# One fused attention-and-mixing kernel on one core: chunk states summed in PSUM, operations over two PSUM banks, and a new list scheduler

## The chip, the cores and the metric

The kernel runs on one core of one Trainium2 chip. The metric is the device time of one execution in microseconds (us), as a median of several runs. Engines are named as in the profile: PE is the matrix engine, PEld its weight loads, DVE the vector engine, ACT the scalar engine, POOL the GpSimd engine, SP the engine that issues most of the transfers. PE's results go to PSUM, a memory of eight banks here; the other tiles lie in SBUF, and an evacuation is a copy from PSUM to SBUF. "Clock" is the mean clock that the throttle granted PE, as a share of full speed; a run whose clock or time puts it in a slower state is labelled slow and is not compared.

## The reference

Two stages, one after the other. The first is a linear-attention recurrence with a decaying state per head, the second mixes tokens and channels.

```
# 4 batches, 8 heads, 768 tokens, head size 48
for t in range(S):
    cur     = outer(u * k[t], v[t])
    y[t]    = r[t] @ (state + cur)              # per head, 48 x 48 state
    state   = w * state + outer(k[t], v[t])
x = y with its heads side by side                # (4, 768, 384)

theta = x @ w_theta                              # 384 x 384
y2 = w_tok_r @ (x * cos(theta)) + w_tok_i @ (x * sin(theta))    # 768 x 768 over tokens
z  = x + y2
out = z + max(z @ w_ch, 0)
```

The recurrence is computed in six chunks of 128 tokens. With r multiplied by powers of w and k by inverse powers, a chunk is a masked product of transposed r and k ("scores", then `mAT`) plus a product with the state at the chunk's start (`Sb`).

## The kernel before

A Python planner (`Plan`) collects tasks with rough durations, orders them for each engine, and gives PSUM banks to them; the instructions are then emitted in that order. The framework adds the semaphore waits by what tiles each instruction touches. The parts that matter here:

```
P = Plan(8)
bank_t = [ps.tile([C, 512], F32, name=f"bank{i}") for i in range(8)]    # eight tiles of one bank

def flip6(dst, blocks, tok, prio, rd, wr):                # transposes on PE, one evacuation on ACT
    def go():
        for i, s in enumerate(blocks):
            nc.tensor.matmul(bank16(tok)[:, i * C:(i + 1) * C], s, ident, is_transpose=True, ...)
    P.add(PE, 55 * n, go, ...)
    P.add(ACT, act_ns(n * C), lambda: nc.scalar.activation(
        dst, bank16(tok)[:, :n * C].rearrange("p (a c) -> p a c", a=n), Act.Copy), ...)

# RT: transposed r of one batch and head pair. Partition p of r holds tokens 6p .. 6p+5,
# so block n of the transposes holds tokens n, n+6, n+12, ...
flip6(RT[:, hp].rearrange("q (p n) -> q n p", n=NCH), [Rw[:, n, 2 * hp:2 * hp + 2, :] for n in range(NCH)], ...)
```

Block n's 128 columns are written to `RT` at steps of six bf16 elements, 12 bytes. The reader of PSUM goes through consecutive elements, the writer of SBUF jumps.

```
# state of each chunk: kept in SBUF as fp32 (Y), updated on DVE, scaled to bf16 (Sb) on POOL
for hp in range(HP):
    nc.vector.scalar_tensor_tensor(Y[:, cc, hp, :], Y[:, cc - 1, hp, :], wC[:, hp:hp + 1],
                                   src[:, hp], op0=Alu.mult, op1=Alu.add)
P.add(POOL, ..., lambda: nc.gpsimd.tensor_mul(Sb[:, cc], Y[:, cc], wide(wC, D)), ...)

# theta, sin, cos, zr, channel product and fin: per chunk of 128 tokens, one bank each
# [... cut ...]

# startup: w broadcast to 128 partitions by a transfer; Ln of w, then Ln of the small wu tile,
# then the powers wpow (Exp), which wait for both
P.add(ACT, 150, lambda: nc.scalar.activation(lw_p, wup[:, :HP], Act.Ln), rd=["wup", "lw_f"], wr=["lw_p"], ...)
P.add(ACT, 500, lambda n=n: nc.scalar.activation(wpow[:, :, n, :], lw_f, Act.Exp, scale=tok_f[:, n:n + 1]),
      rd=["lw_f", "lw_p", "tok_f"], ...)
```

Of the kernel before, what the change touches and what calls it, by code (L numbers as in the profile page):

```python
# [15 lines left out]
F32 = mybir.dt.float32  # L16
# [4 lines left out]

def bc(ap, axis, n):
    new_ap = [list(x) for x in ap.ap]
    new_ap.insert(axis, [0, n])
    return dataclasses.replace(ap, ap=new_ap)


PE, DVE, ACT, POOL, SP = "PE", "DVE", "ACT", "POOL", "SP"


class Task:
    __slots__ = ("eng", "ns", "fn", "deps", "prio", "seq", "lat", "acq", "uses", "nwait",
                 "users", "ready", "end", "mode")


class Plan:



    def __init__(self, nbanks):  # L40
        self.tasks, self.writer, self.readers = [], {}, {}
        self.nbanks = nbanks
        self.bank_uses = {}
        self.bank_of = {}

    def add(self, eng, ns, fn, rd=(), wr=(), prio=0.0, lat=60.0, acq=(), use=(), mode=None):
        t = Task()
        t.eng, t.ns, t.fn, t.prio, t.lat, t.mode = eng, ns, fn, prio, lat, mode
        t.seq = len(self.tasks)
        t.acq, t.uses = list(acq), list(acq) + list(use)  # L50
        rd, wr = list(rd) + list(use), list(wr) + list(acq)
# [19 lines left out]

    def order(self):
# [5 lines left out]
        waiting = {e: [] for e in (PE, DVE, ACT, POOL, SP)}  # L78
        for t in self.tasks:
            if t.nwait == 0:  # L80
                waiting[t.eng].append(t)
        free_at = {e: 0.0 for e in waiting}
        last_mode = None
        banks = [(0.0, i) for i in range(self.nbanks)]
        left = dict(self.bank_uses)
        freed = {}
        out, now, n = [], 0.0, len(self.tasks)
        while len(out) < n:
            for e in waiting:
                while free_at[e] <= now:  # L90
                    nfree = sum(1 for b in banks if b[0] <= now)
                    best = None
                    for t in waiting[e]:
                        if t.ready <= now and len(t.acq) <= nfree:
                            if best is None or (t.prio, t.seq) < (best.prio, best.seq):
                                best = t
# [3 lines left out]
                    waiting[e].remove(t)  # L100
                    banks.sort()
                    for b in t.acq:
                        self.bank_of[b] = banks.pop(0)[1]
                    ns = t.ns
                    if e == PE:
                        if t.mode != last_mode:
                            ns += 100.0
                        last_mode = t.mode
                    free_at[e] = now + ns
                    t.end = now + ns + t.lat  # L110
                    out.append(t)
                    for b in t.uses:
                        left[b] -= 1
                        freed[b] = max(freed.get(b, 0.0), t.end)
                        if left[b] == 0:
                            banks.append((freed[b], self.bank_of[b]))
                    for x in t.users:
                        x.ready = max(x.ready, t.end)
                        x.nwait -= 1
                        if x.nwait == 0:  # L120
                            waiting[x.eng].append(x)
            nxt = [f for f in free_at.values() if f > now]
            nxt += [t.ready for e in waiting for t in waiting[e] if t.ready > now]
            nxt += [b[0] for b in banks if b[0] > now]
# [3 lines left out]
            now = min(nxt)  # L128
        return out


def rows_of(w, n):
    return dataclasses.replace(w, ap=[[0, n]] + [list(x) for x in w.ap])


def wide(ap, n):
    return dataclasses.replace(ap, ap=[list(x) for x in ap.ap] + [[0, n]])


@with_exitstack  # L140
def kernel(
# [13 lines left out]
    nc = tc.nc  # L155
    B, H, S, D = r.shape
# [7 lines left out]
    NS = NCH - 1  # L164
# [4 lines left out]
    bank_t = [ps.tile([C, 512], F32, name=f"bank{i}") for i in range(8)]  # L169

    def bank(tok):
        return bank_t[P.bank_of[tok]]

    def bank16(tok):
        return bank(tok).bitcast(BF16)
# [3 lines left out]


    ident_f = sb.tile([C, C], F32, name="ident_f")
    ident = sb.tile([C, C], BF16, name="ident")
    mask01 = sb.tile([C, C], BF16, name="mask01")
    pi2 = sb.tile([C, 1], F32, name="pi2")
    wu = sb.tile([2 * HP, 2, Dp], F32, name="wu")
    w_f = sb.tile([C, H, D], F32, name="w_f")
    lw_f = sb.tile([C, H, D], F32, name="lw_f")
    lw_p = sb.tile([C, HP], F32, name="lw_p")
    tok_i = sb.tile([C, NCH + 1], mybir.dt.int32, name="tok_i")
    tok_f = sb.tile([C, NCH + 1], F32, name="tok_f")  # L190
    wpow = sb.tile([C, H, NCH, D], F32, name="wpow")
    wpinv = sb.tile([C, H, D], F32, name="wpinv")
    wup = sb.tile([C, 2 * HP], F32, name="wup")
    wC = sb.tile([C, HP], F32, name="wC")
    uw = sb.tile([C, HP, 2], BF16, name="uw")

    NL = 8
    Ls = ring(NL, [C, 2 * HD], F32, "ld")
    r_fs = ring(2, [C, H, NCH * D], F32, "r_f")
    Rws = ring(1, [C, NCH, H, Dp], BF16, "Rw")  # L200
    Kws = ring(4, [C, 2, H, Dp], BF16, "Kw")
    vbs = ring(5, [C, 2, H, D], BF16, "vb")
# [3 lines left out]
    mATs = ring(6, [C, 2, HP, C], BF16, "mAT")  # L206
    Ys = ring(1, [C, NS, HP, D], F32, "Y")
    Sbs = ring(2, [C, NS, HP, D], BF16, "Sb")
    dgs = ring(3, [C, 2 * H], F32, "dg")
    yds = ring(3, [C, 2, H, D], BF16, "yd")  # L210
    xs = ring(3, [C, NCH, HD], BF16, "x")
# [3 lines left out]
    xTs = ring(2, [C, 2, ND, C], BF16, "xT")  # L215
    uns = ring(2, [C, 2, HD], BF16, "un")
    uTs = ring(2, [C, 2, ND, C], BF16, "uT")
# [6 lines left out]
    def act_ns(n, psum=True):  # L224
        return n / 1.2 + (60 if psum else 95)

    def dve_ns(n, rate=1.0):
        return n / (0.96 * rate) + 75

    def pool_ns(n):  # L230
        return 190 + 1.95 * n


    def setup():
        P.add(ACT, 100, lambda: nc.scalar.dma_start(out=w_f, in_=rows_of(w, C)),
              wr=["w_f"], prio=-100, lat=3000)

        def wu_fill():
            nc.vector.memset(wu, 0.5)
        P.add(DVE, 100, wu_fill, wr=["wu"], prio=-100)  # L240

        def wu_load():
            nc.scalar.dma_start(out=wu[:HP, :, :D], in_=w.rearrange("(a b) d -> a b d", b=2))
            nc.scalar.dma_start(out=wu[HP:, :, :D], in_=u.rearrange("(a b) d -> a b d", b=2))
        P.add(ACT, 200, wu_load, wr=["wu"], prio=-99, lat=3000)

        def tok():
            nc.gpsimd.iota(tok_i[:, :NCH], pattern=[[1, NCH]], base=0, channel_multiplier=NCH)
            nc.gpsimd.iota(tok_i[:, NCH:], pattern=[[0, 1]], base=0, channel_multiplier=1)
        P.add(POOL, 400, tok, wr=["tok_i"], prio=-100)  # L250

        def tok2():
            nc.vector.tensor_scalar(tok_i[:, :NCH], tok_i[:, :NCH], C - 1, None,
                                    op0=Alu.bitwise_and)
            nc.vector.tensor_copy(tok_f, tok_i)
            nc.vector.tensor_scalar(tok_f[:, NCH:], tok_f[:, NCH:], -1.0, -1.0,
                                    op0=Alu.mult, op1=Alu.add)
            nc.vector.memset(pi2, math.pi / 2.0)
            nc.vector.memset(uw, 0.0)
        P.add(DVE, 400, tok2, rd=["tok_i"], wr=["tok_f", "uw", "pi2"], prio=-99)  # L260

        def pads(ts):
            for t in ts:
                nc.gpsimd.memset(t[:, :, :, D:], 0.0)
        P.add(POOL, 900, lambda: make_identity(nc, ident_f), wr=["ident_f"], prio=-98)
        P.add(DVE, 200, lambda: nc.vector.tensor_copy(ident, ident_f), rd=["ident_f"],
              wr=["ident"], prio=-98)
        P.add(POOL, 600, lambda: pads(Rws), wr=[("Rw", hp) for hp in range(HP)], prio=-97)
        P.add(POOL, 800, lambda: pads(Kws), wr=[("Kw", i) for i in range(4)], prio=-96)

        def mask():
# [4 lines left out]
        P.add(POOL, 600, mask, wr=["mask"], prio=-95)  # L276

        P.add(ACT, 1800, lambda: nc.scalar.activation(lw_f, w_f, Act.Ln), rd=["w_f"],
              wr=["lw_f"], prio=-98)

        def wu_flip():
            nc.tensor.matmul(bank("wu")[:, :2 * HP], wu.rearrange("p a d -> p (a d)"),  # L282
                             ident_f[:2 * HP, :2 * HP], is_transpose=True,
                             start=True, stop=True)
        P.add(PE, 300, wu_flip, rd=["wu", "ident_f"], acq=["wu"], prio=-90)
        P.add(DVE, 100, lambda: nc.vector.tensor_copy(wup, bank("wu")[:, :2 * HP]),
              use=["wu"], wr=["wup"], prio=-90)
        P.add(ACT, 150, lambda: nc.scalar.activation(lw_p, wup[:, :HP], Act.Ln),
              rd=["wup", "lw_f"], wr=["lw_p"], prio=-97)

        def uw_fill():
# [3 lines left out]
        P.add(DVE, 200, uw_fill, rd=["wup"], wr=["uw"], prio=-90)  # L295
        for n in range(NCH):
            P.add(ACT, 500 + (1300 if n == 0 else 0), lambda n=n: nc.scalar.activation(  # L297
                wpow[:, :, n, :], lw_f, Act.Exp, scale=tok_f[:, n:n + 1]),
                rd=["lw_f", "lw_p", "tok_f"], wr=[("wpow", n)], prio=-96 + 0.1 * n)
        P.add(ACT, 500, lambda: nc.scalar.activation(  # L300
            wpinv, lw_f, Act.Exp, scale=tok_f[:, NCH:]),
            rd=["lw_f", "lw_p", "tok_f"], wr=["wpinv"], prio=-95)
        P.add(ACT, 150, lambda: nc.scalar.activation(wC, lw_p, Act.Exp, scale=float(C)),
              rd=["lw_p"], wr=["wC"], prio=-94)


    nload = [0]

    def slot():
        nload[0] += 1  # L310
# [349 lines left out]
```

## Time and profile before

| | before |
|---|---|
| time, median of 3 runs | 206.19 us (205.81 to 206.32) |
| span in the profile | 204.4 us |
| granted clock | 0.921 |
| PE busy | 145.3 us, 71% |
| DVE, ACT, POOL busy | 124.6, 123.3, 75.1 us |
| 16 RT evacuations | 46.0 us, 2874 ns each |
| first scores start | 26.98 us |

These are lines of the profile page of the kernel before: the busy time of each engine (share of the span, number of instructions), busy tenths in 40 equal slices for PE and ACT and the granted clock in tenths, the chain of waits that ended last (share of the span by engine, then by line), and groups of instructions (output, input, shapes, count, busy us, mean ns of one, idle time before them and its releaser).

```profile
span 204.4 us, 4137 instructions
...
PE 145.3 (71%) x1641; PEld 95.7 (47%) x1641; DVE 124.6 (61%) x260; ACT 123.3 (60%) x165; POOL 75.1 (37%) x73
...
PE   0008178896582897599933988999329989999971
...
ACT  2299987999599706409999433755992327511120
...
PEclk9999999999669589969995899999985999999998
...
PE 41%; ACT 21%; DVE 19%; issue 8%; DMA 8%; POOL 1%; ACTq 0%; POOLq 0%; DVEq 0%; SPq 0%
...
L382 ACT ACTIVATE xT_135<-bank_65 128x768 bf16<-128x768 bf16 x2 | 1.6, 810 | 11.0 <-PE bank_65 L379 11.0
...
L382 ACT ACTIVATE RT_104<-bank_63 128x768 bf16<-128x768 bf16 x2 | 5.9, 2946 | 0.0
```

Read the last two together: the same line of code, engine, operation, types and size, 810 against 2946 ns (all 12 `xT` evacuations take 827 ns on average, all 16 `RT` evacuations 2874). The input pattern is the same; only the output differs, consecutive for `xT` and in steps of 12 bytes for `RT`. The chain has no single owner: ACT has only 21% of it. But the slices show that ACT's 9s and PE's holes go together.

Windows of ten microseconds of the kernel before make that plain. The columns are the window, its length, busy us and number of instructions for PE, PEld, DVE, ACT and POOL, the granted clock, DMA share and GB/s.

```profile
core 0: us, PE busy (x) PEld busy (x) DVE busy (x) ACT busy (x) POOL busy (x), PEclk, DMA share, GB/s
...
20.00:30.00 10.00, 4.38 (x88) 3.59 (x84) 4.15 (x10) 9.77 (x9) 2.31 (x3) 1.00 0.20 74
...
60.00:70.00 10.00, 4.76 (x61) 2.88 (x61) 3.44 (x8) 10.00 (x8) 0.79 (x3) 0.81 1.22 241
...
100.00:110.00 10.00, 3.56 (x71) 2.88 (x68) 5.65 (x11) 10.00 (x5) 7.77 (x7) 0.86 0.76 138
...
140.00:150.00 10.00, 4.99 (x88) 3.99 (x85) 2.89 (x9) 9.58 (x5) 1.01 (x2) 1.00 0.19 72
```

Four times, once for each batch, ACT is full and PE is less than half busy. The first of them also ends the startup. This is the first score matmul in the timeline of the kernel before; the bracket says how long PE was idle and what released it:

```profile
26.98 0.28 PE L438 MATMUL bank_61<-RT_104,KT_106 64*128 64x128 bf16 x1 [5.62 <-ACT KT_106 L382]
```

The ACT queue had four RT evacuations of about 2.9 us in front of that `KT` evacuation.

### The profile page before, as it was taken

The page shows a single profiled execution, that of the slowest core. Times are in us where ns is not written, and L with a number is a line of the kernel's source. Part 1 is how long each engine was busy: PE and PEld are TensorE (multiplying, and loading weights), DVE is VectorE, ACT ScalarE, POOL GpSimd, SP SyncE. Part 2 cuts the span into 40 slices and gives each one's busy share as a digit, 9 for nine tenths or more (in the row PEclk, how much of TensorE's full clock was granted, in tenths as well). Part 3 has the DMA queues.
Part 4 walks back from the last instruction along what each step waited for, and adds up shares of the span by engine and source line. Part 5 has one row for each costly group of instructions (what it writes and reads, how often), then busy time and mean ns, then how long its engine had stood idle before and what let it go on. Part 6 is the DMA issues. An engine that isn't in the chain of part 4 may idle for free.

```text
span 204.4 us, 4137 instructions
## 1 busy us (share of the span) xinstructions
PE 145.3 (71%) x1641; PEld 95.7 (47%) x1641; DVE 124.6 (61%) x260; ACT 123.3 (60%) x165; POOL 75.1 (37%) x73
## 2 busy tenths in 40 slices
PE   0008178896582897599933988999329989999971
PEld 0016165774460555356621755657215655566630
DVE  2028279355740899978861999944419896544442
ACT  2299987999599706409999433755992327511120
POOL 6024121606960489523791083440104082400000
PEclk9999999999669589969995899999985999999998
DMA  4999209999899992829290510022020002022222
GB/s 119 236 230 227 112 6 275 333 332 321 170 198 292 189 167 50 263 69 203 81 195 0 129 29 3 0 82 77 0 77 3 0 3 77 3 77 77 79 80 77
DMA packets 60092, 25.25 MB, mean 124 GB/s; under 512 B 50472, under 2 KB 58536, under 8 KB 60072
## 3 DMA queue, kind: packets, MB, share of 16 engines
q1 hardware_dynamic: 59904, 24.78, 49.9%
q8 instruction: 13, 0.21, 0.5%
q10 hardware_dynamic: 168, 0.20, 0.5%
q14 instruction: 7, 0.06, 0.1%
HBM read 20.25 MB, written 4.72 MB: 122 GB/s over the span
## 4 chain that ended last, share of the span: by engine, by line
PE 41%; ACT 21%; DVE 19%; issue 8%; DMA 8%; POOL 1%; ACTq 0%; POOLq 0%; DVEq 0%; SPq 0%
ACT RT_104 L382 8%; ACT RT_105 L382 7%; DMA r_f_93<-in_r_dram 5%; PE bank_66 L586 5%; PE bank_64 L586 3%; DMA wu<-in_u_dram 3%; PE bank_68 L586 2%; PE bank_63 L586 2%; PE bank_65 L586 2%; DVE Y_116 L494 2%; DVE mAT_114 L443 2%; ACT wpow L297 2%; PE bank_67 L586 1%; PE bank_62 L586 1%; DVE Kw_96 L416 1%
## 5 line engine op out<-in xcount | busy, mean ns | idle before, releaser
L586 PEld LDWEIGHTS <-WrT 128*128 128x128 bf16 x144 | 14.5, 104 | 10.4 <-issue 3.1
L499 POOL TENSOR_TENSOR Sb_118<-Y_116,wC 128x192 bf16<-128x192 f32 x10 | 5.4, 544 | 34.0 <-DVE Y_116 L494 18.6
L586 PEld LDWEIGHTS <-WiT 128*128 128x128 bf16 x144 | 12.8, 98 | 6.8 <-issue 0.5
L397 POOL TENSOR_TENSOR Rw_94<-r_f_92,wpow 128x576 bf16<-128x576 f32 x6 | 10.1, 1713 | 10.1 <-ACT wpow L297 10.1
L397 POOL TENSOR_TENSOR Rw_94<-r_f_93,wpow 128x576 bf16<-128x576 f32 x8 | 12.6, 1600 | 0.4 <-DMA r_f_93<-in_r_dram 0.4
L499 POOL TENSOR_TENSOR Sb_117<-Y_116,wC 128x192 bf16<-128x192 f32 x10 | 6.1, 606 | 16.6 <-DVE Y_116 L494 13.5
L379 PEld LDWEIGHTS <-Rw_94 128*128 128x128 bf16 x96 | 8.0, 120 | 8.6 <-issue 6.2
L438 PEld LDWEIGHTS <-KT_107 64*128 64x128 bf16 x96 | 4.1, 116 | 12.4 <-issue 8.1
L449 DVE TENSOR_TENSOR PD_109<-RT_105,KT_107 128x1024 bf16<-128x1024 bf16 x4 | 3.3, 823 | 10.8 <-ACT RT_105 L382 6.6
L449 DVE TENSOR_TENSOR PD_108<-RT_104,KT_106 128x1024 bf16<-128x1024 bf16 x4 | 4.1, 1030 | 6.8 <-ACT KT_106 L382 6.8
L382 ACT ACTIVATE xT_135<-bank_65 128x768 bf16<-128x768 bf16 x2 | 1.6, 810 | 11.0 <-PE bank_65 L379 11.0
L438 PEld LDWEIGHTS <-KT_106 64*128 64x128 bf16 x96 | 3.8, 117 | 8.6 <-ACT KT_106 L382 5.9
L604 PEld LDWEIGHTS <-uT_138 128*128 128x128 bf16 x36 | 3.5, 108 | 8.9 <-ACT uT_138 L382 6.4
L282 PE MATMUL bank_61<-ident_f,wu 8*128 8x8 f32 x1 | 0.2, 239 | 8.7 <-DMA wu<-in_u_dram 8.7
L604 PEld LDWEIGHTS <-uT_139 128*128 128x128 bf16 x36 | 3.2, 98 | 7.0 <-ACT uT_139 L382 5.3
L382 ACT ACTIVATE RT_104<-bank_65 128x768 bf16<-128x768 bf16 x2 | 5.7, 2844 | 0.4 <-PE bank_65 L379 0.4
L382 ACT ACTIVATE RT_104<-bank_63 128x768 bf16<-128x768 bf16 x2 | 5.9, 2946 | 0.0
L382 ACT ACTIVATE RT_105<-bank_66 128x768 bf16<-128x768 bf16 x2 | 5.7, 2842 | 0.1
L604 PE MATMUL bank_68<-Wch,uT_138 128*128 128x384 bf16 x6 | 1.8, 424 | 5.3 <-ACT uT_138 L382 5.3
L379 PE MATMUL bank_62<-ident,Rw_94 128*128 128x128 bf16 x12 | 1.3, 261 | 5.8 <-DVE Rw_94 L397 5.8
L552 PEld LDWEIGHTS <-xT_134 128*128 128x128 bf16 x36 | 3.5, 106 | 4.1 <-ACT xT_134 L382 2.0
L438 PE MATMUL bank_61<-RT_104,KT_106 64*128 64x128 bf16 x12 | 1.4, 246 | 5.6 <-ACT KT_106 L382 5.6
(540 smaller groups left out, 542.3 us busy)
## 6 DMA issues: line engine op xcount, KB each, us to landing
r_f_92<-in_r_dram SPq DMA_DIRECT2D x2, 1152.0 KB, 7.8
r_f_93<-in_r_dram SPq DMA_DIRECT2D x2, 1152.0 KB, 10.4
out_dram<-fin_140 SPq DMA_DIRECT2D x6, 384.0 KB, 2.4
out_dram<-fin_141 SPq DMA_DIRECT2D x6, 384.0 KB, 2.4
ld_88<-in_k_dram SPq DMA_DIRECT2D x4, 192.0 KB, 6.6
ld_89<-in_v_dram SPq DMA_DIRECT2D x4, 192.0 KB, 3.3
ld_84<-in_k_dram SPq DMA_DIRECT2D x4, 192.0 KB, 5.6
ld_87<-in_moe_w_tok_i_dram SPq DMA_DIRECT2D x2, 384.0 KB, 4.6
```

What stands on the lines that cost most here:

```text
L297: P.add(ACT, 500 + (1300 if n == 0 else 0), lambda n=n: nc.scalar.activation(wpow[:, :, n, :], lw_f, Act.Exp, scale=tok_f[:, n:n + 1]), rd ...
L379: nc.tensor.matmul(bank16(tok)[:, i * C:(i + 1) * C], s, ident, is_transpose=True, start=(i == 0), stop=(i == n - 1))
L382: P.add(ACT, act_ns(n * C), lambda: nc.scalar.activation(dst, bank16(tok)[:, :n * C].rearrange("p (a c) -> p a c", a=n), Act.Copy), use=[t ...
L397: eng.tensor_mul(Rw[:, :, 2 * hp:2 * hp + 2, :D].transpose([0, 2, 1, 3]), rf[:, 2 * hp:2 * hp + 2, :].rearrange("p h (n d) -> p h n d", n= ...
L438: nc.tensor.matmul(bank(tk[hi])[:, hp * C:(hp + 1) * C], KT[q, c, hp, :], RT[q, hp, cc * C:(cc + 1) * C], start=(hp == 0), stop=(hp == HP ...
L443: P.add(DVE, dve_ns(HP * C), lambda hi=hi, tk=tk, mAT=mAT: nc.vector.tensor_mul(mAT[:, hi], bank(tk[hi]).rearrange("p (h t) -> p h t", h=H ...
L449: nc.vector.tensor_mul(PD, RT[:, :, 2 * pr * C:(2 * pr + 2) * C].rearrange("p h (a t) -> p a h t", a=2), KT)
L494: nc.vector.scalar_tensor_tensor(Y[:, cc, hp, :], Y[:, cc - 1, hp, :], wC[:, hp:hp + 1], src[:, hp], op0=Alu.mult, op1=Alu.add)
L499: P.add(POOL, pool_ns(HP * D), lambda cc=cc: nc.gpsimd.tensor_mul(Sb[:, cc], Y[:, cc], wide(wC, D)), rd=[("Y", cc), "wC"], wr=[("Sb", b % ...
L552: nc.tensor.matmul(bank(th)[:, :HD], xT[:, t, dk, :], Wth[:, dk, :], start=(dk == 0), stop=(dk == ND - 1))
L586: nc.tensor.matmul(bank(tm)[:, :HD], WT[:, so, to * C:(to + 1) * C], z[:, so], start=(part == 0 and j == 0), stop=(part == 3 and j == 2))
L604: nc.tensor.matmul(bank(tf)[:, :HD], uT[:, t, dk, :], Wch[:, dk, :], start=(dk == 0), stop=(dk == ND - 1))
```

## The change

The intent: take work off DVE, ACT and POOL so that PE stays busy. In one rewrite:

1. `RT` is written consecutively; the stride moves to the PSUM side of the copy.
2. The states of a pair of chunks are added up in PSUM by matmuls, two heads side by side in one 96-column block; DVE masks out the off-diagonal blocks while it copies (`Sb`). The fp32 state in SBUF and its updates go.
3. PSUM is declared as four tiles of two banks. Mask, x, theta, sin, cos, zr, channel product and fin work over two chunks in two banks at once.
4. A new scheduler plans pairs of banks, gives some tasks to whichever of two engines is free, and keeps POOL and certain DVE operations apart in time. Scaling k goes mostly to POOL.
5. Startup: w comes as one row and is broadcast by a matmul; one set of ACT tables serves Ln and Exp; wpow no longer waits for the wu tile. r of batch 1 is loaded between the two halves of the token weights.

```diff
-    bank_t = [ps.tile([C, 512], F32, name=f"bank{i}") for i in range(8)]
+    banks = [ps.tile([C, 2, 512], F32, name=f"bank{i}") for i in range(4)]
+    def dbl(tok):
+        return banks[P.bank_of[tok] // 2]
     def bank(tok):
-        return bank_t[P.bank_of[tok]]
+        i = P.bank_of[tok]
+        return banks[i // 2][:, i % 2]
 ... (cut)
-            flip6(RT[:, hp].rearrange("q (p n) -> q n p", n=NCH),
+            flips(RT[:, hp].rearrange("q (p n) -> q p n", n=NCH),
                   [Rw[:, n, 2 * hp:2 * hp + 2, :] for n in range(NCH)],
-                  ("TR", b, hp), base + hp, [("Rw", hp)], [("RT", b % 2, hp)])
+                  ("TR", b, hp), base + 0.1 * hp, [("Rw", hp)], [("RT", b % 2, hp)], "RT",
+                  {ACT: act_op(768)}, lambda t: t.transpose([0, 2, 1]))
 ... (cut: states)
-                        nc.vector.scalar_tensor_tensor(
-                            Y[:, cc, hp, :], Y[:, cc - 1, hp, :], wC[:, hp:hp + 1],
-                            src[:, hp], op0=Alu.mult, op1=Alu.add)
-                P.add(POOL, pool_ns(HP * D), lambda cc=cc: nc.gpsimd.tensor_mul(
-                    Sb[:, cc], Y[:, cc], wide(wC, D)), ...)
+                nc.tensor.matmul(bank(tS)[:, :HD], ident, Sb_in..., start=True, stop=False, ...)
+            outer(0, not S_in)          # 4 matmuls of 96 columns into the same bank
+        P.add({DVE: dve_op(HD)}, lambda e: nc.vector.tensor_mul(
+            Sb_mid, bank(tS)[:, :HD].rearrange("p (h e) -> p h e", h=HP), bc(bmask, 1, HP)), ...)
+            P.add({PE: pe_op(170)}, lambda e: outer(1, False), ...)
+            P.add({DVE: dve_op(HD)}, lambda e: nc.vector.tensor_mul(Sb_out, bank(tS)..., wS), ...)
 ... (cut: two banks at once, here theta and zr)
+            for t in range(2):
+                for dk in range(ND):
+                    nc.tensor.matmul(dbl(th)[:, t, :HD], xT[:, ND * t + dk, :], Wth[:, dk, :], ...)
+        P.add({DVE: dve_op(2 * HD)}, lambda e: nc.vector.tensor_mul(
+            zr[:, 2 * pr:2 * pr + 2], dbl(th)[:, :, :HD], x[:, 2 * pr:2 * pr + 2]), ...)
 ... (cut: scheduler, startup)
```

## The prediction

> **What bounds the kernel now.** No single engine. The busy table has PE 145.3 us (71%), DVE 124.6, ACT 123.3, POOL 75.1 of a 204.4 us span; mean granted clock 0.92. Ten-microsecond windows alternate: PE is busy 4.4 us in 20-30, 4.8 in 60-70, 3.6 in 100-110, 5.0 in 140-150, while ACT is busy 9.6 to 10.0 in each. There one batch's transposed r is evacuated. By groups, the 16 RT evacuations take 46.0 us, 2874 ns each; the xT evacuation, same engine, same 768 bf16 elements, 827 ns. RT differs by writing SBUF in steps of six elements (12 bytes). The Trainium skill, "SBUF — State Buffer" (Door 1, cachelines), says accesses that leave a 16-byte line each time pay a penalty; 2874 against 827 ns agrees. The chain of waits carries 14.6% (30 us) on RT evacuations; the rest is startup (first RT evacuation at 15.7 us, after a 6.1 us wu load and a second table load), r of batch 1 landing at 51.5 us (10.4 us), DVE in 73-86 and 112-125, and dense PE from 169 on.
>
> **What changes.**
> 1. RT is written contiguously; the stride (256 bytes) moves to the PSUM read. At one element per cycle: 16 x 0.82 = 13 us, ACT loses 33. No strided PSUM read stands in this trace: the largest risk.
> 2. State in PSUM removes 64 Y updates of 255 ns, 4 copies (17.7 us DVE) and 20 POOL Sb operations (11.5 us); adds 20 DVE multiplies of about 0.5 us and 8 identity matmuls of 0.16. Outer and Sb matmuls fall from 320 to 160 of N=96; PE even to -3 us.
> 3. Pair-wide DVE operations: mask 48x680 ns becomes 24x1.14 us (-5 us); x, zr, fin together -8. Kw scaling (22.4 us DVE, 935 ns mean, 550 alone, so lengthened by POOL) goes mostly to POOL, about 1.8 us each (estimate from Rw's 1.41 us for 576): POOL +17. DVE takes some evacuations from ACT.
> 4. Startup: w comes as one row through PE; wpow no longer waits for wu; one table load fewer before Exp. wpow ready near 9-10 us instead of 13.9, batch 0's RT near 15 instead of 26.
> 5. r of batch 1 loads between halves of the token weights, landing near 33-38 us.
>
> After: DVE 100-115, ACT 80-95, POOL 80-90 us, all below PE.
>
> **The sum.** PE work at full clock, from start-to-start times of dense stretches: mixing 288 x 0.163 = 47; theta and channel 23.5; bf16 transposes 336 x 0.067 = 22.5; fp32 transposes 11; attention 12 pairs x 2 = 24. Sum 128 us. About 25 us pass before PE becomes dense, with 12 us of that done. The remaining 116 us at 90-92% density: 127. Tail 3 us, timed run over span 2. Together 157-159. Counted from before: startup -11, three RT stretches -17, cold clock after them (0.66 to 0.86 in several windows) -8 to -10, DVE-bound stretches and r1 -8: 159-162.
>
> Predicted: 159 us, range 149 to 176. Faster by over 2%: 0.95; within 2%: 0.03; slower: 0.02.
>
> **What would show it.** RT evacuations near 0.8-0.9 us; no window after 30 us with PE under 7 of 10; mean clock above 0.95; PE 125-138 us busy, above 80% of the span; mixing on PE the largest part of the chain; first scores near 15-17 us.
>
> **What would make it wrong.** Strided PSUM reads as slow as the strided writes (then 175-185). Bank pairs: scores take four of eight banks at once, theta, y and channel two, so PE may wait for banks. POOL and two-input DVE operations lengthening each other, now with Kw on POOL. A fixed order with wrong durations stalling in-order queues. A cold clock if small gaps persist.

## The result, and the profile after

| | before | after |
|---|---|---|
| time, median of 4 runs each | 206.25 us | 173.32 us (172.72 to 173.87) |
| ratio of fast runs, 95% interval | | 0.837 (0.833 to 0.842) |
| span in the profile, clock | 204.4 us, 0.921 | 172.2 us, 0.979 |
| PE, DVE busy | 145.3, 124.6 us | 137.9, 113.2 us |
| ACT, POOL busy | 123.3, 75.1 us | 71.6, 76.2 us |
| one RT evacuation | 2874 ns | 815 ns |
| first scores start | 26.98 us | 16.17 us |
| r of batch 1 landed | 51.5 us | 33.1 us |

Ratios here and below are of fast runs, and not quite the ratios of the medians that are quoted. The outputs are right.

The same lines of the profile page, after:

```profile
span 172.2 us, 3640 instructions
...
PE 137.9 (80%) x1491; PEld 96.1 (56%) x1491; DVE 113.2 (66%) x163; ACT 71.6 (42%) x102; POOL 76.2 (44%) x62
...
PE   3056699997969869968699999997899999699970
...
ACT  3966236775953425457633532556105213000000
...
PEclk9999999999999999999969999999999999999995
...
PE 53%; DVE 21%; ACT 11%; issue 7%; DMA 3%; POOL 3%; ACTq 1%; DVEq 0%; POOLq 0%
...
L549 DVE TENSOR_TENSOR mAT<-bank,mask 128x1024 bf16<-128x1024 f32 x24 | 29.0, 1216 | 1.0 <-PE bank L543 1.0
...
L260 ACT ACTIVATE RT<-bank 128x768 bf16<-128x768 bf16 x16 | 12.8, 815 | 9.4 <-PE bank L472 5.5
```

The holes of PE that answered to a full ACT are gone, the clock is nearly full, and RT costs 13 us instead of 46. The same windows of the kernel after:

```profile
20.00:30.00 10.00, 8.91 (x108) 7.05 (x109) 7.42 (x10) 4.48 (x6) 4.96 (x4) 1.00 1.11 343
...
60.00:70.00 10.00, 8.17 (x114) 5.99 (x114) 8.51 (x13) 3.71 (x6) 3.94 (x3) 1.00 1.06 229
...
100.00:110.00 10.00, 9.28 (x102) 6.25 (x102) 7.75 (x10) 4.04 (x5) 5.76 (x4) 1.00 0.12 41
...
140.00:150.00 10.00, 8.62 (x63) 5.00 (x62) 5.89 (x9) 1.58 (x2) 1.63 (x1) 1.00 0.19 67
```

The first score matmuls of the kernel after, in its timeline:

```profile
16.17 1.03 PE L543 MATMUL bank<-RT,KT 64*128 64x128 bf16 x16 [1.31 <-DVE KT L262]
```

What remains is spread thin: PE misses 1 to 2 us in most windows, and no other engine is full in those shown. A part of these gaps looks odd. These are three lines of the timeline of the kernel after (start, duration, both in us), near 147 us:

```profile
146.03 0.96 DVE L655 TENSOR_TENSOR zr<-bank,x 128x768 bf16<-128x768 f32 x1 [0.57 <-ACT bank L652]
146.90 0.55 DVE L683 TENSOR_TENSOR un<-bank,x 128x384 bf16<-128x384 f32 x1
147.50 0.65 PE L677 MATMUL bank<-zr,WrT 128*128 128x384 bf16 x3 [1.17 <-DVE un L683]
```

PE waits 1.17 us for DVE's `un`. These matmuls take `zr` and the token weights and write a bank; they take nothing that `un` makes. In the planner's assignment they write the second bank of the first two-bank tile, while `un` reads the first bank of that tile. Whether such waits cost anything as a whole is the main question of the experiments.

### The profile page after: what moved, and what is told of

Same layout as the page of the kernel before. It is cut to its first block, busy times and chain, and to the rows that moved or that the text cites. A ratio compares the mean times of both kernels' runs of the same rounds, so it can differ in the third digit from the quotient of the medians.

```text
span 172.2 us, 3640 instructions
## 1 busy us (share of the span) xinstructions
PE 137.9 (80%) x1491; PEld 96.1 (56%) x1491; DVE 113.2 (66%) x163; ACT 71.6 (42%) x102; POOL 76.2 (44%) x62
## 4 chain that ended last, share of the span: by engine, by line
PE 53%; DVE 21%; ACT 11%; issue 7%; DMA 3%; POOL 3%; ACTq 1%; DVEq 0%; POOLq 0%
PE bank L677 22%; PE bank L472 8%; PE bank L694 7%; PE bank L645 6%; DVE mAT L549 5%; ACT RT L260 5%; DVE un L683 3%; DMA wu<-in_u_dram 3%; PE bank L626 2%; DVE fin L698 2%; DVE uT L262 2%; POOL zi L658 2%; PE bank L543 2%; DVE xT L262 2%; DVE Sb L601 2%
## 5 line engine op out<-in xcount | busy, mean ns | idle before, releaser
L677 PE MATMUL bank<-zi,WiT 128*128 128x384 bf16 x144 | 29.9, 326 | 3.7 <-DVE Sb L607 1.4
L569 POOL TENSOR_TENSOR yd<-dg,vb 128x768 bf16<-128x768 f32 x12 | 17.6, 1473 | 33.1 <-ACT dg L260 33.1
L677 PE MATMUL bank<-zr,WrT 128*128 128x384 bf16 x144 | 29.6, 326 | 2.9 <-ACT RT L260 1.4
L658 POOL TENSOR_TENSOR zi<-x,sin 128x768 bf16<-128x768 bf16 x12 | 19.9, 1657 | 25.0 <-ACT sin L649 25.0
L549 DVE TENSOR_TENSOR mAT<-bank,mask 128x1024 bf16<-128x1024 f32 x24 | 29.0, 1216 | 1.0 <-PE bank L543 1.0
L519 POOL TENSOR_TENSOR Kw<-ld,wpinv 128x768 bf16<-128x768 f32 x11 | 19.8, 1822 | 11.7 <-ACT RT L260 11.7
L683 DVE TENSOR_TENSOR un<-bank,x 128x384 bf16<-128x384 f32 x24 | 13.2, 555 | 16.4 <-PE bank L677 9.4
L677 PEld LDWEIGHTS <-WrT 128*128 128x128 bf16 x144 | 13.1, 97 | 11.1 <-issue 4.2
L649 ACT ACTIVATE sin<-bank 128x768 bf16<-128x768 f32 x12 | 9.7, 811 | 20.5 <-DVE fin L698 10.6
L260 ACT ACTIVATE RT<-bank 128x768 bf16<-128x768 bf16 x16 | 12.8, 815 | 9.4 <-PE bank L472 5.5
L491 POOL TENSOR_TENSOR Rw<-r_f,wpow 128x576 bf16<-128x576 f32 x12 | 16.6, 1409 | 0.0
L645 PE MATMUL bank<-Wth,xT 128*128 128x384 bf16 x72 | 14.7, 343 | 1.2 <-DVE xT L262 0.9
L694 PE MATMUL bank<-Wch,uT 128*128 128x384 bf16 x72 | 13.7, 327 | 1.4 <-DVE uT L262 1.4
```

Source lines behind the costliest of these rows:

```text
L260: nc.scalar.activation(dst, src, Act.Copy)
L491: eng_of[e].tensor_mul(Rw[:, :, 2 * hp:2 * hp + 2, :D].transpose([0, 2, 1, 3]), rf[:, 2 * hp:2 * hp + 2, :].rearrange("p h (n d) -> p h n ...
L519: eng_of[e].tensor_mul(Kw[:, :, :, :D].rearrange("p a h d -> p (a h) d"), Ls[ik][:, :, :, :D].rearrange("p a h d -> p (a h) d"), wpinv.rea ...
L549: P.add({DVE: dve_op(8 * C)}, lambda e, hi=hi: nc.vector.tensor_mul(mAT[:, hi].rearrange("p a h t -> p (a h) t"), dbl(tk[hi]).rearrange("p ...
L569: P.add({POOL: pool_op(2 * HD, 1.7)}, lambda e: nc.gpsimd.tensor_mul(yd.rearrange("p a (h d) -> p (a h) d", h=H), wide(dg, D), vb.rearrang ...
L645: nc.tensor.matmul(dbl(th)[:, t, :HD], xT[:, ND * t + dk, :], Wth[:, dk, :], start=(dk == 0), stop=(dk == ND - 1))
```

## The experiments

Twelve kernels ran, each with three rounds (four runs with the profiled one) beside the kernel before on the same chip: b1, a1, a2, a3 in a first job (kernel before: 206.67 us), a4, a5, a6, b2 in a second (207.66), b3, a7, c1, c2 in a third (206.63). Names with a are edits of the kernel after, with b of the kernel before, with c of the best version. All results were correct; all runs were fast except two of c1.

| kernel | edit | median us (range) | ratio to before (95%) | profiled span us, clock |
|---|---|---|---|---|
| b1_rt_contig | before, RT written consecutively | 180.11 (179.36 to 181.86) | 0.871 (0.865 to 0.878) | 180.1, 0.944 |
| a1_rt_strided | after, RT written in steps again | 206.85 (205.46 to 207.96) | 0.999 (0.992 to 1.006) | 204.9, 0.919 |
| a2_states_sbuf | after, states in SBUF | 184.45 (184.23 to 185.07) | 0.892 (0.886 to 0.898) | 182.5, 0.966 |
| a3_theta_chan_single | after, theta to zr and channel product per chunk | 183.27 (182.94 to 183.52) | 0.885 (0.880 to 0.890) | 181.6, 0.983 |
| a4_one_psum_tile | after, eight banks as one tile | 161.10 (160.39 to 162.15) | 0.778 (0.772 to 0.783) | 160.0, 0.955 |
| a5_theta_chan_single_one_tile | a3 and a4 together | 157.25 (156.89 to 158.78) | 0.761 (0.755 to 0.768) | 155.2, 0.998 |
| a6_states_sbuf_one_tile | a2 and a4 together | 170.03 (169.82 to 170.62) | 0.821 (0.816 to 0.826) | 168.9, 0.938 |
| b2_rt_startup | b1 and the new startup | 172.67 (172.42 to 173.22) | 0.834 (0.829 to 0.838) | 171.1, 0.954 |
| b3_pair_tiles | b2, its banks declared as four two-bank tiles | 199.72 (199.24 to 200.62) | 0.965 (0.959 to 0.971) | 198.9, 0.957 |
| a7_rt_strided_one_tile | a4, RT written in steps | 181.65 (180.84 to 182.34) | 0.878 (0.872 to 0.884) | 179.1, 0.960 |
| c1_w_bf16 | a5, token weights cast to bf16 before their transposes | 159.05 (156.70 to 159.31) | 0.763 (0.754 to 0.772) | 157.6, 0.957 (slow) |
| c2_replanned | a5, planned with longer hand-overs | 157.09 (156.80 to 157.71) | 0.760 (0.756 to 0.764) | 155.5, 0.988 |

The theories at the start: (A) the RT write is nearly all of the gain, and the missing 14 us are waits that the rest of the rewrite brought in; (B) the states in PSUM and the pair-wide operations carry a good part of the gain themselves; later (C), as the rival of the waits: the wide operations hold two or four of eight banks for long, and a free bank is what PE lacks.

### b1: the RT write alone, in the old kernel

```diff
-            flip6(RT[:, hp].rearrange("q (p n) -> q n p", n=NCH), [...], ...)
+            flip6(RT[:, hp].rearrange("q (p n) -> q p n", n=NCH), [...], ...,
+                  src=lambda t: t.transpose([0, 2, 1]))        # applied to the PSUM operand
```

Expected before the run:

> The kernel before with one thing changed: the evacuation of transposed r writes SBUF contiguously and reads PSUM with the stride (same plan, since the planned cost of 0.7 us stays). Expected: 16 evacuations near 0.82 us each instead of 2.87. If the slow evacuations made most of the loss, as predicted (startup 8 us, three stretches 17 us, cold clock 8 us), 206 goes to 174-181 us. Rival, that the pairs, the states in PSUM and the new order made most of the gain: 192 us or more.

Measured: 180.11 us, 26.5 us less than the kernel before of the same job (206.67), with its order of instructions unchanged. This is the RT group of that run on its profile's group list:

```profile
L382 ACT ACTIVATE RT<-bank 128x768 bf16<-128x768 bf16 x16 | 12.4, 814 | 3.7 <-PE bank L379 3.7
```

814 ns is what a copy of that size takes with both sides consecutive (810 for `xT` above). So reading PSUM at steps of 256 bytes cost ACT nothing that these numbers show. One access pattern gives most of what the whole rewrite gives.

### a1: the RT write undone, in the new kernel

```diff
-            flips(RT[:, hp].rearrange("q (p n) -> q p n", n=NCH), ..., lambda t: t.transpose([0, 2, 1]))
+            flips(RT[:, hp].rearrange("q (p n) -> q n p", n=NCH), ...)
```

> The new kernel with the old strided write of transposed r, plan unchanged. ACT gets 33 us more, of which it has over 90 us free. If RT sits on the critical path of the new kernel as it did in the old one: 8 us at the start and 5 to 8 us in each of three batches, so 195 us or more. Rival, that the idle ACT absorbs it outside the startup: 179-184 us.

Measured: 206.85 us, the same as the kernel before (206.67). Undoing this one line takes away all of the rewrite's 33 us. Its group and chain lines on the profile page:

```profile
PE bank L677 20%; ACT RT L260 17%; PE bank L472 8%; PE bank L694 6%; DVE mAT L549 4%; PE bank L645 3%; DMA wu<-in_u_dram 2%; PE bank L543 2%; PE bank L626 2%; DVE fin L698 2%; DVE un L683 2%; DVE uT L262 2%; POOL zi L658 2%; ACT sin L649 2%; PE bank L621 1%
...
L260 ACT ACTIVATE RT<-bank 128x768 bf16<-128x768 bf16 x16 | 43.2, 2773 | 9.9 <-PE bank L472 5.7
```

RT is 17% of the chain, 35 us of 204.9. Theory A stands for its first half. The loss (33.5 us) is larger than the 30.4 us that ACT works longer (43.2 less 12.8): waits behind the slow copies must add to it. a7 comes back to that.

### a2: the states in SBUF again, in the new kernel

```diff
-                nc.tensor.matmul(bank(tS)[:, :HD], ident, Sb_in..., start=True, stop=False)
-            outer(0, not S_in)
-        P.add({DVE: ...}, lambda e: nc.vector.tensor_mul(Sb_mid, bank(tS)..., bc(bmask, 1, HP)))
+                for hp in range(HP):
+                    nc.vector.scalar_tensor_tensor(Yo[:, hp], Yi[:, hp], wR[:, hp:hp + 1] if c == 0 else 1.0,
+                                                   src[:, hp], op0=Alu.mult, op1=Alu.add)
+            P.add({POOL: pool_op(HD)}, lambda e: nc.gpsimd.tensor_mul(So, Yo, bc(bmask, 1, HP) if c == 0 else wS))
```

> The new kernel with the states kept in SBUF again: one outer product per chunk into its own bank, four DVE multiply-adds of 96 columns per chunk (one copy for the first), one POOL multiply per chunk to bf16; no identity matmul. DVE about +10 us (113 to 123), POOL about +18 us (76 to 94), PE about -3 us. If the states in PSUM are a part of the gain: slower by 3 us or more (over 176). Rival, that DVE and POOL have room and the chain is on PE: within 1.5 us of 173.3.

Measured: 184.45 us, 11.1 us more than the kernel after. The plan was made anew for it, so this compares the two designs, not one instruction. By itself, the step is worth its place.

### a3: theta, sin, cos, zr, channel product and fin per chunk, in the new kernel

```diff
-        th = ("th", g)                                   # two banks, both chunks
-        P.add({ACT: act_op(2 * HD)}, lambda e: nc.scalar.activation(sn, dbl(th)[:, :, :HD], Act.Sin), ...)
+        for t in range(2):
+            th = ("th", g, t)                            # one bank, one chunk
+            P.add({ACT: act_op(HD)}, lambda e, t=t, th=th: nc.scalar.activation(sn[:, t], bank(th)[:, :HD], Act.Sin), ...)
```

> The new kernel with theta, sin, cos, zr and channel, fin per chunk in single banks again (scores, masks and y stay in bank pairs). 48 more operations, about 0.15-0.19 us of overhead each: ACT +5 us, DVE +4 us. If needing two neighbouring free banks is what keeps PE below the predicted density: 171 us or less. Rival, that the pair-wide operations save time: 174-178 us.

Measured: 183.27 us, 10.0 us more than the kernel after and outside both expected ranges; the plan was made anew here too. Taken alone this seems to say that pair-wide operations gain 10 us. It misled: see a5. A hint stood in its group list. ACT stands idle before RT evacuations for 5.2 us in all until DVE's `un` ends, though they neither read nor write anything of `un`:

```profile
L260 ACT ACTIVATE RT<-bank 128x768 bf16<-128x768 bf16 x16 | 12.7, 811 | 11.9 <-DVE un L684 5.2
```

Counting semaphore waits in the compiled programs confirmed the hint. A wait among PE, DVE and ACT was counted as needless if the instruction that it waits for shares no PSUM bank and no other written data with it. The kernel after has 96 such waits of 525, a3 has 176 of 603, a2 has 79 of 601; all are between the two banks of one tile. The kernel b2, with eight one-bank tiles, has none of 755. The totals are all waits for a semaphore of PE, DVE or ACT. These counts stand in no trace. The kept kernels were compiled again: the totals came out the same, and the needless waits of the kernel after as 78 to 111, by whether a wait is put down to all the instructions that one step of the semaphore covers or to the last of them; in a4, a5, a6 and b2 no wait was between two banks.

### a4: the eight banks declared as one tile

The order of instructions, their engines and the banks stay; only the declaration differs, and with it the waits that the framework adds.

```diff
-    banks = [ps.tile([C, 2, 512], F32, name=f"bank{i}") for i in range(4)]
+    allb = ps.tile([C, 8, 512], F32, name="bank")
     def dbl(tok):
-        return banks[P.bank_of[tok] // 2]
+        i = P.bank_of[tok]
+        return allb[:, i:i + 2]
     def bank(tok):
-        i = P.bank_of[tok]
-        return banks[i // 2][:, i % 2]
+        return allb[:, P.bank_of[tok]]
```

> The new kernel with its eight PSUM banks declared as one tile instead of four tiles of two banks; the same instructions in the same order on the same banks, only the semaphore waits differ. In the compiled program of the new kernel 96 of 525 waits among PE, DVE and ACT are for an instruction that touches only the other bank of the pair; here none is. If these waits are what kept PE below the predicted density: 158 to 167 us, and the PE share of the span over 82%. Rival, that the latency of the hand-overs and the fixed order did it: 171 to 174 us.

Measured: 161.10 us, 12.2 us less than the kernel after. Of its 552 waits none is needless in the sense above. The same place as above, in the timeline of a4:

```profile
136.02 0.65 PE L676 MATMUL bank<-zr,WrT 128*128 128x384 bf16 x3
136.35 0.10 PEld L471 LDWEIGHTS <-un 128*128 128x128 bf16 x1
136.76 0.55 DVE L682 TENSOR_TENSOR un<-bank,x 128x384 bf16<-128x384 f32 x1
137.36 0.50 PE L471 MATMUL bank<-ident,un 128*128 128x128 bf16 x6 [0.69 <-DVE un L682]
```

Now the mixing matmuls start 0.74 us before `un` does, with no idle time in front of them. The real wait, that of the transposes of `un` for `un`, is still there and is 0.69 us. This refutes theory C as the main cause: the planned banks are the same in both kernels. (The programs compiled again show the same instructions in the same order on the same banks, for the kernel after and a4 as for the pairs a3 and a5, a2 and a6, b2 and b3.)

The Trainium skill, "PSUM — Partial Sum Buffer" (PSUM bank collisions raise a hardware error), asks for semaphores by bank and quadrant of partitions and says that engines on different banks run clean. This agrees as far as it goes: a4 has no waits between different banks, and its results are correct.

### a5: a3 with one tile

The edit is that of a3 and that of a4 together.

> The variant with theta, sin, cos, zr and channel, fin per chunk in single banks (183.3 us), its banks declared as one tile. It had 176 waits for the other bank only, now 0. If those made its loss of 10 us: within 3 us of the new kernel with one tile, so 160 to 169 us. Rival, that the 48 more operations cost it: 8 to 12 us slower than the new kernel with one tile.

Measured: 157.25 us, 3.9 us less than a4, run in the same job. So the order turns round: per chunk was 10.0 us slower than pair-wide with two-bank tiles, and is faster with one tile. The time is below the expected 160 to 169 us, and the rival, that the 48 more operations cost the time, is refuted. Some of the 3.9 us is granted clock (0.980 to 0.998 against 0.944 to 0.986); the two runs nearest in clock, 0.986 and 0.980, have spans of 158.7 and 156.0 us, so about 2.7 us remain. The plan was made anew, so a4 and a5 differ in the order of instructions too. The page of a5, with the DMA engines' busy tenths and the lines of its chain:

```profile
span 155.2 us, 3716 instructions
...
PE 131.4 (85%) x1491; PEld 92.5 (60%) x1491; DVE 113.0 (73%) x185; ACT 74.9 (48%) x128; POOL 77.3 (50%) x62
...
DMA  4999999999999399999999896022000022022022
...
PE bank L677 25%; SPq L402 11%; PE bank L694 6%; PE bank L471 5%; PE bank L645 4%; DMA ld<-in_v_dram 4%; DVE mAT L548 4%; DMA ld<-in_k_dram 4%; DVE PD L553 3%; ACT sin L649 3%; PE bank L454 2%; DVE zr L655 2%; PE bank L542 2%; DVE un L683 1%; PE bank L625 1%
```

What joining saves on DVE is small: `fin` takes 956 ns for two chunks in the kernel after and 550 for one in b1, so 12 joined operations save 12 x (2 x 550 - 956), 1.7 us in all. Against it, the first chunk's result comes later; that this is what costs the time was not tested by itself.

### a6: a2 with one tile

The edit is that of a2 and that of a4 together.

> The variant with the states in SBUF (184.5 us), its banks declared as one tile; it had 79 waits for the other bank only, now 0. If the states in PSUM are worth something by themselves: still 6 to 12 us slower than the new kernel with one tile. Rival, that its loss came from waits for the other bank: within 3 us of it.

Measured: 170.03 us, 8.9 us more than a4. So the states in PSUM gain also when there are no needless waits. The size is less sure than the sign: a6 ran at a clock of 0.931 to 0.938, a4 at 0.944 to 0.986.

### b2: the new startup in b1

```diff
-        P.add(ACT, 100, lambda: nc.scalar.dma_start(out=w_f, in_=rows_of(w, C)), wr=["w_f"], ...)
+        P.add(ACT, 100, lambda: nc.scalar.dma_start(out=w_row, in_=w.rearrange("(o h) d -> o (h d)", o=1)), ...)
+        P.add(ACT, 0, lambda: nc.scalar.preload_act_table_set("natural_log_exp_and_others"), wr=["table"], ...)
+        P.add(PE, 700, lambda: nc.tensor.matmul(bank("w")[:, :HD], ones, w_row, start=True, stop=True), ...)
-                rd=["lw_f", "lw_p", "tok_f"], wr=[("wpow", n)], ...
+                rd=["lw_f", "tok_f"], wr=[("wpow", n)], ...
```

> The kernel before with contiguous transposed r (180.1 us) and the new startup: w as one row spread by a matmul, one table set loaded at once for Ln and Exp, wpow not waiting for wu. If the startup is worth what the trace of both says (first scores 3 to 5 us earlier): 175 to 177.5 us. Rival, that the loads bound what follows and the time comes back: 179 us or more.

Measured: 172.67 us, 7.4 us less than b1, more than expected. First scores start at 21.29 us in b1 and at 17.07 us in b2, 4.2 us earlier; where the other 3 us come from was not followed up. And 172.67 us is what the kernel after takes (173.32): the old kernel with these two edits equals the rewrite. The states in PSUM, the wide operations and the scheduler together netted nothing as shipped.

The Trainium skill, "ScalarE: Activation LUTs" (What ACT_TABLE_LOAD costs, and its table of sets), gives about 1283 ns for a load, and names a set with both exp and ln. The traces agree: each load takes 1.28 us, the kernel before has two before its first Exp (for Ln and for Exp), the kernel after one.

### b3: two-bank tiles in b2, and nothing else

```diff
-    bank_t = [ps.tile([C, 512], F32, name=f"bank{i}") for i in range(8)]
+    bank_t = [ps.tile([C, 2, 512], F32, name=f"bank{i}") for i in range(4)]
     def bank(tok):
-        return bank_t[P.bank_of[tok]]
+        i = P.bank_of[tok]
+        return bank_t[i // 2][:, i % 2]
```

> The kernel before with contiguous r and the new startup (172.7 us), its eight banks declared as four tiles of two banks, nothing else: the same instructions, order and banks, no operation two banks wide. Its program now has 192 of 703 waits for the other bank of a pair only (0 before). If such waits cost time by themselves: slower by 10 us or more, 183 us and up. Rival, that they cost only together with operations two banks wide: within 2 us of 172.7.

Measured: 199.72 us, 27 us more than b2, from a declaration alone; no operation is wide here. 192 of its 703 waits are needless. The pages of b2 and b3, their busy lines:

```profile
PE 138.4 (81%) x1643; PEld 92.4 (54%) x1643; DVE 122.9 (72%) x261; ACT 92.5 (54%) x164; POOL 73.3 (43%) x73
```

```profile
PE 148.8 (75%) x1643; PEld 96.6 (49%) x1643; DVE 123.6 (62%) x261; ACT 95.0 (48%) x164; POOL 73.1 (37%) x73
```

The number of instructions of each engine is equal, and DVE, ACT and POOL work equally long within 3%. All of them are merely spread over 28 us more. PE's record is 10 us busier with the same matmuls; why was not followed up. So the mechanism holds in the old kernel as in the new one.

### a7: a4 with the strided RT write

The edit is that of a1 in a4.

> The new kernel with one PSUM tile (161.1 us) and the old strided write of r, plan unchanged. The strided write cost 33.5 us in the new kernel with pair tiles and 26.5 us in the old one. If the waits for the other bank enlarged its cost: 180 to 188 us here. Rival, that the cost of four evacuations of 2.9 us in a row is the same in every version: 190 us or more.

Measured: 181.65 us, 20.5 us more than a4. In the kernel after, the same edit cost 33.5 us. So 13 us of what a1 lost were not the slow copy itself but came with the declaration, that is with needless waits behind the copy:

| RT write | two-bank tiles | one tile |
|---|---|---|
| in steps of 12 bytes | 206.85 us | 181.65 us |
| consecutive | 173.32 us | 161.10 us |

The four times are from four jobs, whose kernels before lie within 1.4 us of each other. The slow copy and the declaration are not additive: with two-bank tiles, a long instruction on one bank also holds up whoever wants the other bank.

### c1: less PE work in a5

```diff
+                P.add({ACT: act_op(S, False)}, lambda e, ...: copy(e, st, flat(i)[:, :S]), ..., name="Wcast")
-                            nc.tensor.matmul(dbl(tok)[:, g, j * C:(j + 1) * C], flat(i)[:, o:o + C], ident_f, is_transpose=True, ...)
+                        nc.tensor.matmul(bank16(tok)[:, j * C:(j + 1) * C], st[:, j * C:(j + 1) * C], ident, is_transpose=True, ...)
```

> The fastest version so far (theta and channel per chunk, one PSUM tile, 157.25 us) with the token weights cast to bf16 on ACT before they are transposed: 12 casts of 0.84 us on ACT, 72 transposes in bf16 (0.34 us per six instead of 0.66), so 3.9 us less PE work. If the kernel is now bound by PE work: 152.5 to 154.5 us. Rival, that it is bound by hand-overs between engines, PE being idle 15% of the span: 156 to 158 us.

Measured: 159.05 us; its two fast runs took 158.89 and 156.70 us, the other two, labelled slow, 159.31 and 159.22. The two fast runs lie on both sides of the upper edge of the rival's range (156 to 158). Inconclusive. The ratio to the kernel before, of fast runs, does not differ from a5's. But a clock of 0.955 to 0.959 in all four runs, against 0.98 to 1.00 in a5, hides what less PE work would give at the same clock: PE was busy for 131.1 us, as in a5 (131.4), in spite of 3.9 us less work planned. What can be said: in this form it isn't a gain.

### c2: a5 planned with longer hand-overs

```diff
 def dve_op(n, rate=1.0):
-    return (n / (0.96 * rate) + 70, 115)
+    return (n / (0.96 * rate) + 70, 215)        # likewise for PE, ACT and POOL: 100 ns more each
-        P.add({SP: (1000, 2000)}, lambda e: nc.sync.dma_start(out=out[...], in_=fin), ...)
+        P.add({ACT: (60, 2000)}, lambda e: nc.scalar.dma_start(out=out[...], in_=fin), ...)
```

> The fastest version so far (157.25 us), planned with 0.1 us more latency for every hand-over, and with the output DMAs issued by ACT, so that loads never stand behind an output that is not ready. If the optimistic plan and the blocked load queue still cost something: 153 to 156 us. Rival, that they cost nothing any more: 156.5 us or more.

Measured: 157.09 us, the same as a5. The two changes together gain nothing; they were made in one run, so that one gains what the other loses is not excluded. a5 and c2 are the fastest versions found, 157.1 to 157.3 us, faster than both kernels.

## Why the prediction was right or wrong

The time, 173.32 us, lies in the range (149 to 176), near its upper end, and 14 us above the 159 predicted. That it lies inside is owed to the range's width, 17 us upward, and not to a cost that was foreseen: the one risk with a price, slow strided PSUM reads (175 to 185), didn't happen, and what did happen had no price.

**The RT write: right in cause, and a little smaller than it was counted.** 2874 ns became 815 (predicted 0.8 to 0.9 us), the strided PSUM read was not slow, and ACT's holes in PE went. The Trainium skill, "SBUF — State Buffer" (Door 1, the note on cachelines), says that accesses to a new 16-byte line each time pay a penalty; with steps of 12 bytes, three writes of four go to a new line, so the trace of before agreed. b1 now shows by the one edit that the strided write was the cost; no run tried another step, so that the line is the reason is not shown. The same note says that any non-contiguous PSUM pattern slows matmuls; for a read of PSUM by ACT, which it doesn't speak of, b1 shows no slowing. The prediction split the consequences into startup (11), RT stretches (17) and clock (8 to 10), 36 to 38 us together. b1 and b2 measured 26.5 for RT and 7.4 more for the startup, 33.9 us.

**The startup: right.** First scores at 16.17 us (15 to 17 predicted), 10.8 us earlier than before (11), batch 0's last RT evacuation at about 15.4 (15), r of batch 1 landed at 33.1 (33 to 38).

**The clock: right.** 0.979 (above 0.95).

**The work of the engines: right for PE and DVE.** PE 137.9 us busy (125 to 138), 80% of the span (above 80%), mixing the largest part of the chain; DVE 113.2 (100 to 115). Of the ten-microsecond windows between 30 and 160 us none has PE under 7.68 of 10 (none under 7 predicted). ACT was at 71.6 rather than 80 to 95, since DVE took more of the evacuations, and POOL at 76.2 rather than 80 to 90.

**The density: wrong, and this is the step that failed.** The sum said: "The remaining 116 us at 90-92% density: 127." Keep the prediction's own sum of PE work, 128 us, which is an estimate: PE's busy time can't check it, for the same instructions are busy for 137.9 us in the kernel after and 133.3 us in a4. In the kernel after PE was busy for 13 us by 25 us; with that and a tail of 3, the other 115 us of work took 172.2 - 28 = 144.2 us: 80%. In a4, with the same instructions in the same order on the same banks, it took 160.0 - 28 = 132.0 us, 87%; in a5, 155.2 - 28 = 127.2 us, 90%. The declaration of the banks accounts for 12.2 of the 14 us (a4: 161.10), and a4 is 2 us above the 159 predicted. So the prediction read the kernel as the programmer meant it. It missed that a tile of two banks ties whatever works on one bank to whatever works on the other.

**"Bank pairs: ... PE may wait for banks": the right place, another mechanism, no price.** The listed risk was a lack of free banks. What the runs show is waiting for the other bank of the same tile (a4, b3). It stood in the list of what could go wrong and not in the sum.

**States in PSUM: right in direction.** 8.9 us with one tile (a6), 11.1 with two-bank tiles (a2), each time between two plans and not by one edit.

**Pair-wide operations: wrong for the second half of them.** For theta, sin, cos, zr, channel product and fin the prediction counted only DVE time saved. At two-bank tiles the wide form is 10.0 us faster (a3), but the narrow form has 176 needless waits instead of 96; without any, the narrow form is some 3 us faster (a5). The wide mask and x were not undone separately; what they are worth is open.

**Where the gain of the rewrite went.** RT and startup in the old kernel give 172.67 us. The rest of the rewrite is worth about 11.6 us more with one tile (a4, 161.10), and the two-bank tiles took 12.2 us away. Nothing was left: 173.32, where the prediction had counted 8 us for DVE-bound stretches and r of batch 1. The earlier load of r, the scaling of k on POOL and the scheduler itself were not undone one by one.

Open: what limits a5 and c2 at 157 us. PE is 85% busy; about 10 of the missing 24 us lie in the first 20 us, the rest in later gaps. The record has a lead that no run followed: the chains of a5 and c2 begin with 16 to 18 us of SP issuing loads one after another (SPq L402, 11%) and one load of over 6 us, and the DMA engines are at 90% or more in nearly every slice of a5's first 85 us. c2 took only the outputs off that queue. c1 didn't settle whether less PE work would help. Also open: why the framework separates the banks of one eight-bank tile but not those of a two-bank tile; only the waits in the compiled programs were seen.

## What to carry to other kernels

A large rewrite can owe its gain to one line: try each part alone in the old kernel before giving credit to the design; here an access pattern and a new startup gave as much as the whole rewrite did. When operations are joined over two PSUM banks, look in the trace for waits between instructions that share no data, and compare declaring the banks as one tile: the same program took 12 to 27 us less without them. And test a design choice again when such a confounder is gone: pair-wide against per-chunk changed its sign.

## What the Trainium skill lacked or had wrong

- "PSUM — Partial Sum Buffer": it rightly says that engines on different banks run clean, but no page says that declaring two banks as one tile makes the framework put waits between them. Measured: 96 of 525 waits and 12.2 us in the kernel after (a4), 192 of 703 waits and 27 us in the old one (b3). A tile of all eight banks, or eight tiles of one bank, had none.
- "SBUF — State Buffer", Door 1: it states a penalty for leaving the 16-byte line, without a size for ACT. Measured: a copy of 768 bf16 elements for each partition, PSUM to SBUF, takes 810 to 815 ns written consecutively, and 2773 to 2874 ns on average written in steps of 12 bytes, 3.4 to 3.5 times as long.
- "SBUF — State Buffer" and "PSUM — Partial Sum Buffer" warn of non-contiguous PSUM patterns for matmuls; neither gives a time for such reads by ACT. Measured: reading PSUM in steps of 256 bytes, 768 bf16 elements, 814 ns, no slower than consecutive (810 to 827).
- No page weighs what an operation over two banks saves against its later result: 951 to 956 ns for 768 elements against about 550 for 384 on DVE saves about 150 ns an operation, and still the version with the wide theta and channel stages took about 3 us longer (a4 against a5); no run here separates the reasons.
